# First-stage Fourier calls of later batches, placed behind the group steps of their unit

## The chip, the cores and the metric

The kernel runs on one core of one Trainium2 chip. The metric is the device time of one execution in microseconds (us). Before the change three runs took 1579.62, 1581.74 and 1581.88 us; their median is 1581.74 us.

Engines are called PE (matrix multiply), PEld (its weight load), DVE (vector), ACT (scalar and activation), POOL and SP. SP here only issues DMA transfers, and a DMA waits in its issuer's queue behind everything that was issued before it; the same holds for the few transfers that ACT issues.

## What is computed

The reference takes x (8 batches of 3072 x 256) through three parts, shortened here:

```
X = rfft(x, axis=1)                        # per batch, over 3072
Y = X @ (w_r + i*w_i) + (b_r + i*b_i)      # complex mix of the 256 columns
Y = soft_threshold(Y, 0.01)                # real and imaginary part
y = irfft(Y)                               # back to 3072 x 256 per batch
r = relu(y @ w_in);  z = (s*r*r + b) @ w_out          # 256 -> 2048 -> 256
logits = z @ w_gate;  e = argmax(logits)              # 8 experts, capacity 768 each
out[i] = softmax_weight * (relu(z_i @ w1[e]) @ w2[e]) # kept rows; other rows are zero
```

## The kernel before

**Loops and units.** The main part runs one loop per batch, b = 0 to 7, of 64 *units* each (k = 0 to 63). A unit (`s_unit`, from line 746) does one sixteenth-part of the first wide product of one eighth of batch b: four matmuls `ph` (L755), a relu on ACT into `r` (L760) and a square on DVE into `qb` (L761). Its PSUM tile comes from a pool "h" of two buffers. After each unit the kernel runs the list of small pieces that stands at that unit in a table (`slot`). The order of the pieces in a unit's list is the order in which the program put them there, so PE, ACT and SP meet them in that order, and each of these engines works strictly in order.

**The pieces.** While loop b multiplies batch b, the pieces bring the next batches through the Fourier part.

- *First-stage calls* (`f1_mm`, 8 per batch) belong to batch b+2 and are in loops 0 to 5. One call is four matmuls `pz` (L237; eight records in the trace, as each is split in two), which take a tile of the same pool "h"; an ACT copy to `z` (L241); four stores `zd` of 96 KB from SP (L245); and two loads of x of 192 KB from SP (L221) for the call two further on. The last two calls of loop 5 load no x. Eight calls for batch 1 are in loop 0 as well, at even units from 6.
- *Group steps* (`group_items`) belong to batch b+1. The first piece loads two `zp` (L265, 256 KB from SP). After it, steps of two kinds alternate: one loads the next `zp`, mixes (`pmx`, L358), thresholds on DVE and multiplies back (`pi`, L394, then a copy `v` on ACT and a store `vd` that ACT issues); the other mixes (`pmx`) and transforms (`pf`, L276, which reads `zp`). In loops 1 to 6 the first piece is at unit 0, the second (loads only) at unit 2, the first `pf` at unit 3, and the steps go on at every second or third unit to unit 50. The steps of units 46 and 50 hold nothing, that of unit 48 only the `pi`. In loop 0 they are at units 24 to 52.
- *Inverse pieces* (`i2_items`) are at units 8i+4 and 8i+5: they read `u` (L403, 384 KB from SP), multiply (`pi`, L415), and store `ad` (L435) from SP. The first two `u` of the next batch are loaded at unit 53 and the first is used at unit 57 (INV0_AT).
- At units 8i+2 there is a logit product `lg` (L775, L778), at units 8i+4 a transpose `plt` (L799), and every fifth unit SP issues a store of zeros to `out` (L1927).

**What sets the order.** No scheduler: the numbers F1_AT, GROUPS_FROM, GROUPS_TO, INV_LOAD_AT and the order of the `put` calls (lines 1896 to 1916) decide it. `put(at, items, per)` puts item n at unit int(at + n*per). Before the change, with F1_AT = 2, the calls of loops 1 to 5 are at units 2, 9, 17, 25, 33, 40, 48, 56 and those of loop 0 at 24, 29, ... 59; they are put in before the group steps of the same unit.

Of the kernel before, what the change touches and what calls it, by code (L numbers as in the profile page):

```python
# [132 lines left out]
GROUPS_TO = 50  # L133
INV_LOAD_AT = 53
INV0_AT = (57, 57, 61)
F1_AT = 2
ZERO_AT = tuple(range(5, 65, 5))
LOGIT_LAG = 3
FIRST_LAG = 13
# [12 lines left out]
class Kern:  # L152
# [1608 lines left out]
    def run(self):  # L1761
        tc, nc, B = self.tc, self.nc, self.B
# [4 lines left out]
        with ExitStack() as es, tc.manual_schedule():  # L1767
# [79 lines left out]
            def fetch(m):  # L1847
                t = self.wk.tile([128, 2, C], F32, tag=("kw", "kw2")[m % 2], name="ga", bufs=1)
                src = self.ad.rearrange("(k j a q g) c -> g j a k q c", j=2, a=4, q=4, g=NK * B)
                for j in range(2):  # L1850
                    for a in range(4):
                        nc.sync.dma_start(out=t[32 * a:32 * a + 32, j], in_=src[m, j, a])
                ga[m] = [t[:, j] for j in range(2)]
# [4 lines left out]
            for b in range(B):  # L1858
# [35 lines left out]
                def put(at, items, per=1.0):  # L1894
                    for n, f in enumerate(items):
                        slot.setdefault(int(at + n * per), []).append(f)
                if b + 1 < B:
                    if b == 0:
                        put(4, [lambda c=c: self.x_ahead(8 + c) for c in range(XP)], 0.5)
                        put(6, self.f1_items(1), 2)  # L1900
                    if b + 2 < B:
                        at = F1_AT if b else 24
                        put(at, self.f1_items(b + 2), (64 - at) / 8)
                    gi = self.group_items(b + 1)
                    s0 = GROUPS_FROM if b else 26
                    put(s0 - 2, gi[:1])
                    ge = GROUPS_TO if b else 52
                    put(s0, gi[1:], (ge - s0) / (len(gi) - 2))
                    put(INV_LOAD_AT, [lambda: self.i2_load(b + 1, 0), lambda: self.i2_load(b + 1, 1)], 0)
                    for at, f in zip(INV0_AT, self.i2_items(b + 1, 0)):  # L1910
                        put(at, [f])
                for i in range(7):
                    if i < 6:
                        put(8 * i, [lambda i=i: self.i2_load(b, i + 2)])
                    for at, f in zip(INV_AT, self.i2_items(b, i + 1)):
                        put(8 * i + at, [f])
                if b == 1:
                    for m, i in enumerate(XB_AT):
                        put(8 * i, [lambda m=m: fetch(m)])
# [70 lines left out]
```

## Time and profile before

| | before |
|---|---|
| median of three runs | 1581.74 us |
| the profiled execution | 1585.16 us |
| its span in the trace | 1583.1 us |
| PE busy | 1423.6 us (90%), 9725 instructions |
| DVE busy | 944.8 us (60%) |
| ACT busy | 793.1 us (50%) |
| POOL busy | 266.8 us (17%) |
| mean DMA rate | 145 GB/s |
| calls of `pz` (L237) | 480 records, 73.5 us busy |

The profile page gives busy times by engine and by group; the trace below it gives every instruction with its start, and, in brackets, how long its engine had been idle in front of it and which instruction ended that. Times in the trace count from the start of the span. The profiled execution is 2.06 us longer than its span. Loop 1 of the kernel runs from about 327 us to 552 us (it holds more work than the others), loop 2 to 706, loop 3 to 848, loop 4 to 991, loop 5 to 1133 us.

### The profile page before, as it was taken

To read this page: it belongs to the slowest core of one execution; us is meant where nothing else is said; L and a number is where in the kernel's file an instruction comes from. 1 tells how busy PE (TensorE), PEld (TensorE's weight loads), DVE (VectorE), ACT (ScalarE), POOL (GpSimd) and SP (SyncE) were. 2 spreads that over 40 slices of the span, in tenths; PEclk is the share of its full clock that TensorE was granted. 3 is DMA by queue.
4 is the path that set the end of the run, shared out by engine and by line. 5 is a ranking of instruction groups with operands and counts; after the bars stand their busy time and mean duration, and the time that the engine had idled before them with its cause. 6 is when DMAs were issued, how large, how long until landed. Compare 5 with 4: busy or idle time off the path is not lost.

```text
span 1583.1 us, 26459 instructions
## 1 busy us (share of the span) xinstructions
PE 1423.6 (90%) x9725; PEld 1195.4 (76%) x9725; DVE 944.8 (60%) x2078; ACT 793.1 (50%) x1196; POOL 266.8 (17%) x235
## 2 busy tenths in 40 slices
PE   5996869999998889999999999999999978998974
PEld 3985648878777668778877887888789867988863
DVE  1776427756554687757666675766677685552410
ACT  1334534465444545575557556655745675642311
POOL 0444200000000002212001201200120152223020
PEclk8898879999999999999999999999999999999987
DMA  7726566584444446466547555554543456530052
GB/s 207 243 87 196 143 181 172 153 218 134 146 140 126 129 128 160 126 168 161 160 117 200 143 144 163 151 164 127 156 118 109 119 148 195 158 94 21 11 198 99
DMA packets 270291, 230.03 MB, mean 145 GB/s; under 512 B 122526, under 2 KB 230816, under 8 KB 270145
## 3 DMA queue, kind: packets, MB, share of 16 engines
q1 hardware_dynamic: 252352, 200.14, 45.6%
q10 hardware_dynamic: 13968, 25.20, 4.5%
q0 software_dynamic: 3824, 2.82, 0.7%
q8 instruction: 81, 1.33, 0.4%
q14 instruction: 66, 0.53, 0.1%
HBM read 114.18 MB, written 114.09 MB: 144 GB/s over the span
## 4 chain that ended last, share of the span: by engine, by line
PE 69%; DVE 10%; ACT 6%; DMA 5%; issue 4%; SPq 2%; POOL 1%; another core or an unknown queue 1%; ACTq 0%; POOLq 0%; DVEq 0%
PE ph L755 16%; PE pmx L358 15%; PE pi L415 5%; PE pf L276 5%; PE pi L394 4%; PE pz L237 4%; PE phx L972 3%; ACT r L760 3%; PE lg L775 3%; PE ya L1434 2%; PE ph L1481 2%; DVE qb L761 2%; PE plt L799 2%; PE ya L987 1%; PE po L1491 1%
## 5 line engine op out<-in xcount | busy, mean ns | idle before, releaser
L755 PE MATMUL ph<-ah,win 128*128 128x384 f32 (+1 forms) x2048 | 449.1, 352 | 16.8 <-ACT r L760 13.6
L760 ACT ACTIVATE r<-ph 128x768 bf16<-128x768 f32 (+1 forms) x512 | 388.1, 784 | 146.8 <-PE ph L755 89.5
L761 DVE TENSOR_TENSOR qb<-r 128x768 bf16<-128x768 bf16 (+1 forms) x512 | 281.5, 554 | 211.7 <-ACT r L760 201.3
L755 PEld LDWEIGHTS ph<-ah,win 128*128 128x128 f32 x2048 | 339.6, 191 | 74.7 <-ACT r L760 44.4
L358 PE MATMUL pmx<-wm,l 128*128 128x256 f32 x1196 | 296.4, 387 | 10.4 <-DVE at L431 5.5
L358 PEld LDWEIGHTS pmx<-wm,l 128*128 128x128 f32 x1196 | 223.0, 192 | 53.5 <-DVE at L431 8.2
L421 POOL TENSOR_TENSOR asq<-ah 128x768 bf16<-128x768 f32 x64 | 96.7, 1511 | 968.7 <-ACT ah L417 888.5
L415 PE MATMUL pi<-f1t,u 96*128 96x96 f32 x1024 | 134.3, 283 | 6.5 <-DMA u<-vd 3.5
L415 PEld LDWEIGHTS pi<-f1t,u 96*128 96x128 f32 x1024 | 130.8, 198 | 11.5 <-issue 5.8
L284 ACT COPY l<-pf 128x512 f32<-128x512 f32 x84 | 49.2, 586 | 152.2 <-PE pf L276 145.2
L396 ACT COPY v<-pi 128x512 f32<-128x512 f32 x96 | 56.4, 588 | 100.6 <-PE pi L394 97.9
L276 PEld LDWEIGHTS pf<-d,zp 128*128 128x128 f32 x672 | 89.6, 195 | 15.2 <-issue 8.2
L394 PE MATMUL pi<-t,e 128*128 128x256 f32 x384 | 99.2, 381 | 0.7 <-DVE t L353 0.7
L276 PE MATMUL pf<-d,zp 128*128 128x128 f32 x672 | 90.6, 279 | 10.3 <-DMA zp<-zd 10.3
L237 PE MATMUL pz<-x,f 48*64 48x512 f32 x480 | 73.5, 645 | 17.8 <-ACT r L760 9.3
L417 ACT CAST ah<-pi 128x384 fp32r<-128x384 f32 x128 | 61.0, 479 | 52.8 <-PE pi L415 51.8
L431 DVE STREAM_TRANSPOSE at<-pi 128x384 f32<-128x384 f32 x128 | 74.2, 580 | 20.3 <-ACT ah L417 12.9
L394 PEld LDWEIGHTS pi<-t,e 128*128 128x128 f32 x384 | 72.3, 190 | 15.1 <-DVE qb L761 3.2
L909 POOL DMA_INDIRECT list<-c,x x64 | 65.5, 1024 | 80.9 <-DVE c L905 64.7
L285 DVE TENSOR_TENSOR l<-pf,l 128x256 f32<-128x256 f32 x84 | 35.6, 424 | 68.8 <-ACT l L284 65.9
L353 DVE TENSOR_TENSOR t<-t,cl 128x512 f32<-128x512 f32 x96 | 73.4, 765 | 3.3
L241 ACT COPY z<-pz 128x1024 f32<-128x1024 f32 x56 | 56.7, 1012 | 29.4 <-PE pz L237 16.9
(409 smaller groups left out, 1826.1 us busy)
## 6 DMA issues: line engine op xcount, KB each, us to landing
zd<-z SPq DMA_DIRECT2D x256, 96.0 KB
zp<-zd SPq DMA_DIRECT2D x96, 256.0 KB
vd<-v ACTq DMA_DIRECT2D x96, 256.0 KB
u<-vd SPq DMA_DIRECT2D x64, 384.0 KB
ad<-at SPq DMA_DIRECT2D x256, 96.0 KB
out<-zero SPq DMA_DIRECT2D x96, 256.0 KB
x<-x SPq DMA_DIRECT2D x120, 192.0 KB
sd<-stage SPq DMA_DIRECT2D x32, 256.0 KB
```

The costliest lines, as they stand in the source:

```text
L237: nc.tensor.matmul(ps[r][64 * k:64 * k + 64, :], self.f1[h], xs[k][h].rearrange("p a c -> p (a c)"), start=True, stop=True, skip_group_che ...
L276: nc.tensor.matmul(pv[:, h, :, gi * 64:gi * 64 + 64], zp[:, gi, h * 128:(h + 1) * 128], self.d[:, 2 * p + gi, :].rearrange("p (t m) -> p t ...
L353: nc.vector.tensor_tensor(out=t, in0=t, in1=cl, op=ALU.subtract)
L358: self.nc.tensor.matmul(o, part(h), w[:, h], start=start and h == 0, stop=stop and h == 1, skip_group_check=True)
L394: nc.tensor.matmul(ps[:, gi * C:(gi + 1) * C], self.e[:, 2 * p + gi], t[:, gi * C:(gi + 1) * C], start=True, stop=True)
L415: nc.tensor.matmul(ps[:, :TC].rearrange("p (a n) -> p a n", n=4)[:, :, n], u[:, n, h::2], self.f1t, start=True, stop=True)
L421: nc.gpsimd.tensor_tensor(out=self.asq[b, i], in0=af, in1=af, op=ALU.mult)
L431: nc.vector.transpose(out=self.ar[:, :, :, h], in_=self.at.pop((b, i, h))[:, :TC].rearrange("p (g c) -> p g c", c=32))
L755: nc.tensor.matmul(ps[:, j, :n], self.win[:, k, f], ah[:, k, t0:], start=(k == 0), stop=(k == 1))
L760: nc.scalar.activation(out=r, in_=ps[:, :, :n], func=AF.Relu)
L761: nc.vector.tensor_tensor(out=q, in0=r, in1=r, op=ALU.mult)
L909: self.nc.gpsimd.indirect_dma_start(out=self.lists[n], out_offset=bass.IndirectOffsetOnAxis(ap=x[:, n:n + 1], axis=0), in_=c[:, n:n + 1], ...
```

## The change

F1_AT becomes a list of eight units, the calls are put in after all other pieces of the unit, and loop 0 keeps its units (24, 29, ... 59) but has the calls behind the other pieces too. Counts and shapes stay as they are. In loops 1 to 5 a call goes from unit 2, 9, 17, 25, 33, 40, 48, 56 to unit 3, 10, 18, 25, 31, 38, 45, 50.

```diff
-F1_AT = 2
+F1_AT = (3, 10, 18, 25, 31, 38, 45, 50)
...
                     if b == 0:
                         put(4, [lambda c=c: self.x_ahead(8 + c) for c in range(XP)], 0.5)
                         put(6, self.f1_items(1), 2)
-                    if b + 2 < B:
-                        at = F1_AT if b else 24
-                        put(at, self.f1_items(b + 2), (64 - at) / 8)
                     gi = self.group_items(b + 1)
...
                     for at, f in zip(INV_AT, self.i2_items(b, i + 1)):
                         put(8 * i + at, [f])
+                if b + 2 < B:
+                    for at, f in zip(F1_AT if b else range(24, 64, 5), self.f1_items(b + 2)):
+                        put(at, [f])
```

On PE, in the later loops around units 32 to 34 (`ph` of two units in one row; `pmx` and `pi` are of the group steps, `pz` is the call):

```order
 L358 MATMUL pmx<-wm_152,l 128x256 x2
 L394 MATMUL pi_6253<-t,e 128x256 x2
-L755 MATMUL ph<-ah,win 128x384 x8
-L237 MATMUL pz<-x,f_108 64x512 x4
+L237 MATMUL pz<-x,f_108 64x512 x4
+L755 MATMUL ph<-ah,win 128x384 x8
 L358 MATMUL pmx<-wm_151,l 128x256 x2
 L358 MATMUL pmx<-wm_150,l 128x256 x2
```

The call stood behind two units and in front of the mixes of a step; now it stands behind the `pi` of the step of unit 31 and in front of the two units.

On SP in loop 0, about unit 24, before (the stores `zd` and loads `x` are those of a call, `zp` the first loads of the group steps):

```order
L1927 DMA out<-zero 256x1x256
L435 DMA ad<-at 32x12x64 x4
L245 DMA zd<-z 48x2x256 x4
L221 DMA x<-x 48x1024 x2
L265 DMA zp<-zd 128x512 x2
L403 DMA u<-vd_84 96x4x256
```

and after:

```order
L1927 DMA out<-zero 256x1x256
L435 DMA ad<-at 32x12x64 x4
L265 DMA zp<-zd 128x512 x2
L403 DMA u<-vd_84 96x4x256
L245 DMA zd<-z 48x2x256 x4
L221 DMA x<-x 48x1024 x2
```

The six transfers of the call went from in front of the `zp` loads to behind them and behind the load of `u`.

On SP in loop 3, units 45 to 53, before (the last row is the load of the first two `u` of the next batch):

```order
L435 DMA ad<-at 32x12x64 x4
L1927 DMA out<-zero 256x1x256
L245 DMA zd<-z 48x2x256 x4
L221 DMA x<-x 48x1024 x2
L1927 DMA out<-zero 256x1x256
L403 DMA u<-vd_88 96x4x256 x2
```

and after:

```order
L435 DMA ad<-at 32x12x64 x4
L245 DMA zd<-z 48x2x256 x4
L221 DMA x<-x 48x1024 x2
L1927 DMA out<-zero 256x1x256
L245 DMA zd<-z 48x2x256 x4
L221 DMA x<-x 48x1024 x2
L1927 DMA out<-zero 256x1x256
L403 DMA u<-vd_88 96x4x256 x2
```

The call that stood behind the two `u` loads (unit 56) is now in front of them, so the transfers of two calls instead of one lie between `ad` and `u`.

## Rows read from the trace of the kernel before

**Rows 1.** Stretches: microseconds, then busy time (count) per engine, granted clock, DMA share, GB/s.

```profile
706.00:848.00 142.00, 137.57 (x919) 114.88 (x918) 95.45 (x205) 85.02 (x121) 20.02 (x16) 1.00 0.58 156
828.00:832.00 4.00, 4.00 (x37) 3.07 (x35) 1.21 (x3) 3.54 (x6) 0.00 (x0) 1.00 0.91 253
```

**Rows 2.** PE timeline, loop 5: start, duration, engine, line, operation; idle in brackets.

```profile
1044.60 1.75 PE L755 MATMUL ph<-ah,win 128*128 128x384 f32 x8
1046.19 1.89 PE L358 MATMUL pmx<-wm,l 128*128 128x256 f32 x8
1047.92 1.05 PE L276 MATMUL pf<-d,zp 128*128 128x128 f32 x8
...
1088.86 1.74 PE L755 MATMUL ph<-ah,win 128*128 128x384 f32 x8
1091.15 1.09 PE L237 MATMUL pz<-x,f 48*64 48x512 f32 x8 [0.55 <-ACT r L760]
1092.17 1.99 PE L358 MATMUL pmx<-wm,l 128*128 128x256 f32 x8
1094.00 1.05 PE L276 MATMUL pf<-d,zp 128*128 128x128 f32 x8
```

**Rows 3.** PE timeline, unit 17 of loop 3, and two units together in loop 4.

```profile
744.98 0.94 PE L755 MATMUL ph<-ah,win 128*128 128x384 f32 x4
...
747.67 1.03 PE L358 MATMUL pmx<-wm,l 128*128 128x256 f32 x4
...
861.16 1.64 PE L755 MATMUL ph<-ah,win 128*128 128x384 f32 x8
862.63 1.03 PE L358 MATMUL pmx<-wm,l 128*128 128x256 f32 x4
```

**Rows 4.** Timelines of SP (SPq) and PE at units 0 to 3 of loops 1, 2, 3.

```profile
330.95 0.96 SPq L265 DMA_DIRECT2D zp<-zd  x2
333.93 1.16 PE L276 MATMUL pf<-d,zp 128*128 128x128 f32 x8 [1.57 <-DMA zp<-zd]
...
552.34 0.97 SPq L265 DMA_DIRECT2D zp<-zd  x2
557.19 1.05 PE L276 MATMUL pf<-d,zp 128*128 128x128 f32 x8
...
707.84 0.97 SPq L265 DMA_DIRECT2D zp<-zd  x2
708.56 1.09 PE L237 MATMUL pz<-x,f 48*64 48x512 f32 x8 [0.19 <-ACT r L760]
709.58 0.83 PE L775 MATMUL lg<-qb,wogd 128*32 128x384 bf16 x16
711.31 1.05 PE L276 MATMUL pf<-d,zp 128*128 128x128 f32 x8
```

**Rows 5.** PE timeline: a wait at unit 48 of loop 3, one at unit 25 of loop 5.

```profile
824.83 0.96 PE L755 MATMUL ph<-ah,win 128*128 128x384 f32 x4 [0.55 <-ACT r L760]
...
1050.58 1.09 PE L237 MATMUL pz<-x,f 48*64 48x512 f32 x8 [0.21 <-ACT r L760]
```

**Rows 6.** Timelines of SP and PE in loop 0, about unit 24.

```profile
217.90 1.88 SPq L245 DMA_DIRECT2D zd<-z  x4
...
220.79 0.90 SPq L265 DMA_DIRECT2D zp<-zd  x2
...
225.16 2.04 PE L276 MATMUL pf<-d,zp 128*128 128x128 f32 x8 [8.03 <-DMA zp<-zd]
```

**Rows 7.** Timelines of SP and PE, units 48 to 57 of loops 3 and 4.

```profile
828.77 2.73 SPq L245 DMA_DIRECT2D zd<-z  x4
832.25 0.80 SPq L221 DMA_DIRECT2D x<-x  x2
833.73 1.12 SPq L403 DMA_DIRECT2D u<-vd  x2
839.53 2.01 PE L415 MATMUL pi<-f1t,u 96*128 96x96 f32 x16
...
976.58 1.11 SPq L403 DMA_DIRECT2D u<-vd  x2
982.71 1.51 PE L415 MATMUL pi<-f1t,u 96*128 96x96 f32 x11 [1.28 <-DMA u<-vd]
```

## The prediction

> **What bounds the kernel now.** I read the busy times by engine first, then one loop of the later batches as a stretch. In loop 3 PE is busy for 137.57 of 142 us at a granted clock of 1.00 (2.4 GHz), ACT and DVE for 85 and 95 us [rows 1]. So PE's own order of work sets the pace: what a change of order is worth is what it does to the seams between PE's pieces and to the few waits that PE still has. The reader should look for two things in the PE timeline: how much later the next piece starts when a call stands in a place, and the bracket in front of an instruction.
>
> A call costs PE more than its own stream. In loop 5 two units, a mix and the next transform take 1047.92 − 1044.60 = 3.32 us from the first `ph` to `pf`; with a call between the units and the mix it is 1094.00 − 1088.86 = 5.14 us, of which 0.55 is a wait for ACT [rows 2]. So the call costs 5.14 − 0.55 − 3.32 = 1.27 us, though from `pz` to the next piece it is only 1092.17 − 1091.15 = 1.02. The rest lies in its seams: the mix behind it lasts 1.83 to the next start, against 1.73, and the `ph` in front of it gives way later. Between two units, where the unit holds no step, the call costs (747.67 − 744.98) − (862.63 − 861.16) = 2.69 − 1.47 = 1.22 us [rows 3]. In front of the logit product it is 709.58 − 708.56 = 1.02 [rows 4].
>
> **The change, part by part.** Durations are those of the profiled execution, so the sum is made against its 1583.1 us of span and 1585.16 us in all (2.06 us lie around the span), 3.42 us above the median of the three runs. The differences are then applied to the median.
>
> *Seams, loops 1 to 5.* Before, four of the eight calls stand in front of a step's matmuls (units 25, 33, 40, 48), three between units (9, 17, 56), and one in front of `lg` (unit 2): 4 × 1.27 + 3 × 1.22 + 1.02 = 9.76 us. After, all stand behind their step: five in front of the next unit's `ph` (3, 25, 31, 38, 45) and three in front of `lg` (10, 18, 50): 5 × 1.22 + 3 × 1.02 = 9.16. The trace has no call behind a `pf` or a `pi`; nearest are the two seams just named. The saving is 0.6 per loop, 3.0 us in five loops. Bounds: nothing, if the seam to the step costs the same from its other side, and 9.76 − 8 × 1.02 = 1.6 per loop if a call costs 1.02 everywhere, so 0 to 8 us. I take 3.0, since it is made of measured seams.
>
> *The wait for ACT at a call.* A call takes a buffer of the pool that the units use, and must wait until the relu of the unit two before is done. These waits are 0.19 at unit 2 [rows 4], 0.21 at unit 25 [rows 5] and 0.55 where two or three units come close together [rows 2, 5]; with 0.55 at units 33, 40 and 48, and 0.2 at unit 56 as at 2 and 25, that is 0.19 + 0.21 + 3 × 0.55 + 0.2 = 2.25 per loop. After, a call directly behind a step has the step's matmuls as cover for the relu, but the two units behind it come one call earlier to their own buffers. I take 0.40, the middle of 0.21 and 0.55, at three units (31, 38, 45), 0.55 at unit 50 and 0.20 once: 1.95, a gain of 0.3 per loop, 1.5 us in all. Bounds per loop: +1.5 if all of the old waits return and the copy of `z` delays the next relu besides, and −2.25 if all go.
>
> *Loop 0.* The units stay, only the order within them turns. The largest single wait here is PE's 8.03 us for the first `zp` [rows 6]. Its load is issued at 220.79, behind the four stores and two loads of the call at unit 24, which begin at 217.90. After the change it takes their place: 220.79 − 217.90 = 2.9 us sooner, and PE ends its wait that much sooner, if nothing but `zp` holds it. Five of the eight calls lie in units with a step's matmuls; at 0.12 each for the seam that is 0.6. Sum −3.5 us; bounds 0 (the time is lost again later, since the next `zp` loads keep PE waiting) and −5 (the load also lands faster: it takes 225.16 − 220.79 = 4.37 us here against 2.98 below).
>
> *The first `zp` of a loop.* Where a call goes away in front of unit 3, PE comes there sooner, and the load does not. In loop 1 it takes 333.93 − 330.95 = 2.98 us and PE already waits 1.57 [rows 4]: all of the 1.02 that the call gave as cover is added. In loop 3 PE arrives 711.31 − 707.84 = 3.47 us behind the issue, without a wait: 0.49 to spare; without the call at unit 2 (1.02, and its wait of 0.19) it arrives 1.21 sooner and waits 1.21 − 0.49 = 0.72. Loops 4 and 5 have the same places; I take 0.72 for each. Loop 2 has 557.19 − 552.34 = 4.85 us and so room for it. Sum 1.02 + 3 × 0.72 = +3.2 us; bounds 0 (the load lands sooner when no call stores beside it) and 6 (five times 1.21).
>
> *The loads of `u` at unit 53.* Now the transfers of the call of unit 50 stand in front of them, and those of the call of unit 45 too, so six more than before: four `zd` and two x. In loop 3 the two loads are issued at 833.73 and PE's `pi` starts at 839.53 without a wait, 5.80 us later; in loop 4 the same takes 982.71 − 976.58 = 6.13 and PE already waits 1.28 [rows 7]. What the room in loop 3 is cannot be seen; from nothing to 5.80 − 2.98, the time of the smaller load. I take 0.5, since loop 4 lies so near. How much later are the loads issued? Upper end: four stores at 2.73 and two loads at 0.80, with short gaps, 3.6 us. Lower end: nothing, if SP has time between its rows, for it mostly waits for `z`. I take 2.0: SP has gaps (its stores end at 828.77 + 2.73 = 831.50, and the next row begins at 832.25), and the first call's six fall partly into them. Loops 2 and 3: 2.0 − 0.5 = 1.5 each; loop 4: all 2.0; loop 5, whose last two calls load no x: 0.5; loop 1, where PE has more work before unit 57: nothing. Sum +5.5 us; bounds 0 and 12.
>
> The Trainium skill, "DMA: Bandwidth & Descriptors", section "Issuing engines are not separate DMA queues", says that all DMAs run on the same 16 engines and interleave. What the rows show that bears on it is that in the four us in which these transfers run the DMA share is 0.91 at 253 GB/s, against 0.58 in the loop [rows 1]. [...]
>
> Sum: −3.0 − 1.5 − 3.5 + 3.2 + 5.5 = +0.7 us. Span 1583.8, profiled execution 1585.9, median 1582.4.
>
> **The rivals.**
>
> *A. The `u` loads land in time: faster.* SP issues the first call's six transfers while it would have waited for the second call's `z`, and the room in loops 2 to 5 takes the rest. For it: SP's queue is not full, and no wait at `pi` is seen in loop 3. Against it: loop 4 waits already. Then the 5.5 fall away: −4.8 us, 1576.9.
>
> *B. The `u` loads are late by the full six transfers: slower.* The place is the first `pi` at unit 57 in loops 2 to 5, the price 3.6 − 0.5 = 3.1 in loops 2 and 3, 3.6 in loop 4 and 2.2 in loop 5, together 12.0 instead of 5.5: +7.2 us, 1588.9. It decides from a delay of about 2.8 us on; below that the sum stays within a measurement's reach. For it: the crowded DMA in that stretch. Against it: SP's gaps.
>
> *C. The change doesn't do what it says: the seams cost the same on either side of a step.* Then the 3.0 are not had: +3.7 us, 1585.4. For it: the mix behind a call lasts 0.10 longer, so it is the change of the shape that costs, and that comes twice at any place. Against it: the calls between units are cheaper than those in front of a mix. The Trainium skill, "TensorE: Matmul & The Clock Gate", section "The mechanism", says that a weight load overlaps a running matmul only where the row groups differ, which would make the seam a matter of the shapes; the 1.22 and 1.27 are near enough to agree, the 1.02 in front of `lg` isn't.
>
> **How the numbers follow.** A measurement of this kernel tells about 0.2%, 3.2 us, from no change: the bounds are 1578.6 and 1584.9. Forecast 0.42, rival A 0.32, rival B 0.17, rival C 0.09. Of the forecast's cases, with its terms a few us off in either direction, 0.03 count as faster and 0.02 as slower; of C 0.04 count as no change. Faster: 0.32 + 0.03 = 0.35. Slower: 0.17 + 0.05 + 0.02 = 0.24. No change: 0.41. The range reaches from A with another 1.4 us of seams or waits gone, 1575.5, to B, 1588.9, since both hold much of the chance. The forecast's own range is 1579 to 1586.
>
> **What would show it.** In the changed profile: `pf` at unit 3 waits about 2.6 us for `zp` in loop 1 and 0.7 in loops 3 to 5; the wait in loop 0 is about 5.1 instead of 8.03; the calls in front of `lg` cost 1.02 with no dearer seam at the step; `pi` at unit 57 waits 1.5 us for `u` in loops 2 and 3 and about 3.3 in loop 4. The forecast is wrong if the `u` load is not waited for (A), if its wait is over 3 us in each loop (B), if the loop 0 gain is given back to the next `zp`, or if the waits for ACT at the calls grow instead of falling.

## The result, and the profile after

| | before | after |
|---|---|---|
| median of five runs | 1581.68 us | 1597.19 us |
| range of the runs | 1579.62 to 1581.88 | 1594.50 to 1601.28 |
| span of the profiled execution | 1583.1 us | 1592.7 us |
| PE waits for `u` (L415), whole execution | 3.5 us in 2 places | 10.3 us in 5 places |

The change makes the kernel slower: the ratio to before is 1.0113, interval 1.0089 to 1.0137. The forecast was 1582.4 with a range to 1588.9, so the time lies outside the range, on the side of rival B and beyond it.

The most useful view is a ledger: the start of the same `ph` (first of a unit) in both traces, and by how much the difference of the two grows in each stretch.

| stretch | forecast, us | traces, us |
|---|---|---|
| loop 0 up to unit 57 | −3.5 | −5.1 |
| loop 0, units 57 to 60 | 0 | +3.1 |
| units 0 to 4, loops 1 to 5 (`zp`) | +3.2 | +6.4 |
| units 4 to 14, loops 1 to 5 | 0 | +2.9 |
| units 14 to 57 (in loop 1 to 60; seams, waits for ACT) | −4.5 | −3.1 |
| units 57 to 60, loops 2 to 5 (`u`) | +5.5 | +12.4 |
| loops 6 and 7 | 0 | −1.8 |
| together, to unit 60 of loop 7 | +0.7 | +14.8 |

The spans differ by only 9.6 us, since the stretch behind unit 60 of loop 7, which the change doesn't touch, took 183.9 us in the profiled execution of before and 178.6 after; over the kernels below it is anything from 176.8 to 183.9, so this difference lies within the scatter. The 14.8 up to there agrees with the medians, which differ by 15.5. Two more entries are scatter, at least in part: 0.8 of loop 0's 5.1 us are there at unit 24 already, before the first call that changed its place, and loops 6 and 7 hold no moved call.

Units 50 to 60 of loop 3 after, first SP's issues and then PE; they answer to [rows 7].

```profile
831.85 1.91 SPq L435 DMA_DIRECT2D ad<-at  x4
833.86 2.36 SPq L245 DMA_DIRECT2D zd<-z  x4
836.32 1.15 SPq L221 DMA_DIRECT2D x<-x  x2
...
838.16 2.01 SPq L245 DMA_DIRECT2D zd<-z  x4
840.26 0.85 SPq L221 DMA_DIRECT2D x<-x  x2
...
841.74 1.16 SPq L403 DMA_DIRECT2D u<-vd  x2
...
844.62 0.96 PE L755 MATMUL ph<-ah,win 128*128 128x384 f32 x4 [0.19 <-ACT r L760]
847.25 2.33 PE L415 MATMUL pi<-f1t,u 96*128 96x96 f32 x16 [1.67 <-DMA u<-vd]
849.28 1.63 PE L755 MATMUL ph<-ah,win 128*128 128x384 f32 x4
850.84 1.47 PE L775 MATMUL lg<-qb,wogd 128*32 128x384 bf16 x16
```

Two calls' transfers stand ahead of `u`, and `pi` waits 1.67 us where it waited for nothing. The two rows below it are the surprise: four `ph` matmuls take 1.63 us and the logit product 1.47, which elsewhere take 0.94 to 0.97 and 0.83 [rows 3, 4, 5]. PE runs at half rate there. The stretches show it (columns as in [rows 1]): first loop 3 before, behind its `pi`, and the stretch behind loop 4's wait of 1.28 us,

```profile
842.00:845.00 3.00, 3.00 (x33) 2.25 (x31) 1.17 (x3) 2.63 (x5) 1.64 (x1) 1.00 0.82 216
...
985.00:988.00 3.00, 3.00 (x32) 2.23 (x31) 1.12 (x2) 2.63 (x4) 1.38 (x1) 1.00 0.87 241
```

and after, behind the waits of loops 3, 2, 4 and 0:

```profile
849.00:852.00 3.00, 3.00 (x23) 2.01 (x24) 0.80 (x2) 1.29 (x2) 0.00 (x0) 0.50 0.31 104
702.00:705.00 3.00, 3.00 (x22) 2.15 (x24) 0.58 (x1) 1.47 (x3) 0.00 (x0) 0.53 0.21 69
997.00:1000.00 3.00, 3.00 (x18) 2.35 (x21) 0.58 (x1) 0.97 (x3) 0.00 (x0) 0.50 0.07 23
316.00:319.00 3.00, 3.00 (x17) 2.79 (x16) 0.58 (x1) 0.96 (x2) 0.00 (x0) 0.58 1.09 299
```

The granted clock is 1.00 (2.4 GHz) before and about 0.5 (1.2 GHz) after. Read in stretches of 2 us from 300 to 1160 us, the time lost to a lower clock (the sum of 2 us times one minus the granted clock) is 5.1 us in three falls before and 13.7 us in eight falls after. They come in equal steps: one fall loses 1.7 us. The same sum from the start to unit 60 of loop 7 is 41.0 us before and 49.5 after, so of the 14.8 us lost, 8.5 are the clock's.

The first `pf` of loops 0, 1 and 3, which answer to [rows 6] and [rows 4]:

```profile
220.16 2.05 PE L276 MATMUL pf<-d,zp 128*128 128x128 f32 x8 [3.83 <-DMA zp<-zd]
...
332.20 1.16 PE L276 MATMUL pf<-d,zp 128*128 128x128 f32 x8 [2.92 <-DMA zp<-zd]
333.30 1.81 PE L237 MATMUL pz<-x,f 48*64 48x512 f32 x8
...
715.72 1.16 PE L276 MATMUL pf<-d,zp 128*128 128x128 f32 x8 [0.86 <-DMA zp<-zd]
```

Loop 0's wait fell from 8.03 to 3.83 us, more than forecast (2.9). In loop 1 the wait grew from 1.57 to 2.92, and `pz` behind it lasts 1.81 instead of 1.09: the clock again. In loop 3 a wait of 0.86 is new.

A wait that nobody had foreseen is at unit 10 of loop 3:

```profile
729.12 0.94 PE L755 MATMUL ph<-ah,win 128*128 128x384 f32 x4
730.95 1.97 PE L358 MATMUL pmx<-wm,l 128*128 128x256 f32 x8 [0.89 <-DVE t L382]
```

The call that stood at unit 9 was cover for DVE, which must finish with a tile before this mix can start; a run below tests that.

The seams, at unit 31 of loop 3 after, which answer to [rows 2, 3]:

```profile
789.60 1.03 PE L394 MATMUL pi<-t,e 128*128 128x256 f32 x4
790.56 1.09 PE L237 MATMUL pz<-x,f 48*64 48x512 f32 x8
791.58 0.97 PE L755 MATMUL ph<-ah,win 128*128 128x384 f32 x4
793.13 0.97 PE L755 MATMUL ph<-ah,win 128*128 128x384 f32 x4 [0.58 <-ACT z L241]
793.93 1.89 PE L358 MATMUL pmx<-wm,l 128*128 128x256 f32 x8
```

The call itself no longer waits, but the second unit behind it now waits for ACT's copy of `z`, 0.58 us. And from `pi` to `ph` it takes 791.58 − 789.60 = 1.98 us, where without a call it is 1088.86 − 1088.18 = 0.68, in loop 5 of before:

```profile
1088.18 1.03 PE L394 MATMUL pi<-t,e 128*128 128x256 f32 x4
1088.86 1.74 PE L755 MATMUL ph<-ah,win 128*128 128x384 f32 x8
```

The call costs 1.30 behind a `pi`, as much as the 1.27 in front of a mix.

### The profile page after: what moved, and what is told of

It reads as the page before. It is cut to its first block, busy times and chain, and to the rows that moved or that the text cites. A ratio compares the mean times of both kernels' runs of the same rounds, so it can differ in the third digit from the quotient of the medians.

```text
span 1592.7 us, 26452 instructions
## 1 busy us (share of the span) xinstructions
PE 1434.4 (90%) x9725; PEld 1199.5 (75%) x9725; DVE 949.3 (60%) x2078; ACT 795.1 (50%) x1196; POOL 264.3 (17%) x235
## 5 line engine op out<-in xcount | busy, mean ns | idle before, releaser
L755 PE MATMUL ph<-ah,win 128*128 128x384 f32 (+1 forms) x2048 | 454.3, 356 | 16.4 <-ACT r L760 9.6
L755 PEld LDWEIGHTS ph<-ah,win 128*128 128x128 f32 x2048 | 343.3, 194 | 90.6 <-ACT r L760 30.7
L415 PE MATMUL pi<-f1t,u 96*128 96x96 f32 x1024 | 137.5, 287 | 13.3 <-DMA u<-vd 10.3
L415 PEld LDWEIGHTS pi<-f1t,u 96*128 96x128 f32 x1024 | 133.6, 202 | 19.0 <-issue 7.1
L276 PEld LDWEIGHTS pf<-d,zp 128*128 128x128 f32 x672 | 88.5, 193 | 17.1 <-DMA zp<-zd 8.9
L431 DVE STREAM_TRANSPOSE at<-pi 128x384 f32<-128x384 f32 x128 | 74.2, 580 | 29.0 <-DMA ad<-at 13.7
```

The lines of the kernel that those rows point to most:

```text
L276: nc.tensor.matmul(pv[:, h, :, gi * 64:gi * 64 + 64], zp[:, gi, h * 128:(h + 1) * 128], self.d[:, 2 * p + gi, :].rearrange("p (t m) -> p t ...
L415: nc.tensor.matmul(ps[:, :TC].rearrange("p (a n) -> p a n", n=4)[:, :, n], u[:, n, h::2], self.f1t, start=True, stop=True)
L431: nc.vector.transpose(out=self.ar[:, :, :, h], in_=self.at.pop((b, i, h))[:, :TC].rearrange("p (g c) -> p g c", c=32))
L755: nc.tensor.matmul(ps[:, j, :n], self.win[:, k, f], ah[:, k, t0:], start=(k == 0), stop=(k == 1))
```

## The experiments

Two theories were set against each other first: that the new places cost (P), or that standing behind a step costs (O). All ratios are to the kernel before on the same chip; there were three sets, with medians of before of 1582.08, 1584.07 and 1576.64 us. The expected times were written with a before of about 1582 us in mind; where before took another time, above all in the third set, a result is held against them by its ratio.

**Order alone.** The calls behind, at the units of before:

```diff
-F1_AT = (3, 10, 18, 25, 31, 38, 45, 50)
+F1_AT = (2, 9, 17, 25, 33, 40, 48, 56)
```

> The calls stand behind the other pieces of their unit, as after the change, but in loops 1 to 5 at the units of before (2, 9, 17, 25, 33, 40, 48, 56). Theory P (the places cost, not the order within a unit): the waits for zp at unit 3 and for u at unit 57 in loops 1 to 5 are those of before, loop 0 keeps what it has after the change (about 2 us less than before), and the median is 1578 to 1582. Rival O (standing behind a step costs, by dearer seams and later stores): the loss stays, 1590 to 1598.

Measured: 1574.37 us, ratio 0.9941 (0.9925 to 0.9958). O falls; the order is even a gain, and more than P had it. In the trace there is no wait for `u` in loops 1 to 5 and none for `zp` in loops 2 to 5; loop 4's 1.28 of before is gone as well:

```profile
974.56 0.97 PE L755 MATMUL ph<-ah,win 128*128 128x384 f32 x4
975.37 2.01 PE L415 MATMUL pi<-f1t,u 96*128 96x96 f32 x16
```

**Place alone.** The list of new units in before's position:

```diff
-F1_AT = 2
+F1_AT = (3, 10, 18, 25, 31, 38, 45, 50)
...
-                        at = F1_AT if b else 24
-                        put(at, self.f1_items(b + 2), (64 - at) / 8)
+                        for at, f in zip(F1_AT if b else range(24, 64, 5), self.f1_items(b + 2)):
+                            put(at, [f])
```

> The calls stand in front of the other pieces of their unit, as before the change, but in loops 1 to 5 at the new units (3, 10, 18, 25, 31, 38, 45, 50); loop 0 is as before. Theory P: PE waits for u at unit 57 in loops 2 to 4 as after the change (1.7 to 3 us), and for zp at unit 3 less, since the call is in front of pf there and covers about 1 us; 1590 to 1597. Rival O: about as before, 1580 to 1584.

Measured: 1587.36, ratio 1.0030 (1.0009 to 1.0050). The interval corresponds to 1583 to 1590, between O's times and P's: the loss is smaller than P had it, but the kernel is slower than before, as P says. The waits for `u` were shorter than P had them, 0.72, 0.44 and 1.99 us in loops 2 to 4; only the longest was followed by a low clock. So the places cost, and more so together with the new order.

**The loads of `u` first.**

```diff
-                    put(INV_LOAD_AT, [lambda: self.i2_load(b + 1, 0), lambda: self.i2_load(b + 1, 1)], 0)
+                    put(50 if b else INV_LOAD_AT, [lambda: self.i2_load(b + 1, 0), lambda: self.i2_load(b + 1, 1)], 0)
```

> As after the change, but in loops 1 to 6 the two loads of u are issued at unit 50 instead of 53, in front of the stores and loads of the call at unit 50. Theory Q (SP's queue order delays u): the waits at unit 57 in loops 2 to 4 go, and with them the low granted clock behind them, 3.5 to 4.8 us in each of these loops; 1583 to 1587. Rival V (the transfers' volume delays u, wherever they stand in the queue): u still lands late, 1591 to 1597.

Measured: 1586.82, ratio 1.0033 (1.0014 to 1.0051), 0.8% below the changed kernel's 1.0113. SP at unit 50 of loop 3 and PE at unit 57:

```profile
826.12 2.37 SPq L245 DMA_DIRECT2D zd<-z  x4
...
830.35 1.11 SPq L403 DMA_DIRECT2D u<-vd  x2
831.55 1.97 SPq L245 DMA_DIRECT2D zd<-z  x4
...
837.71 2.01 PE L415 MATMUL pi<-f1t,u 96*128 96x96 f32 x16
839.50 0.94 PE L755 MATMUL ph<-ah,win 128*128 128x384 f32 x4
```

`pi` has no wait and the `ph` behind it is at full rate, though the same transfers run in the same microseconds (a share of 1.01 from 830 to 836 us): it is the place in SP's queue, theory Q, not the volume alone. The loads also moved from unit 53 to 50, but SP's own time explains the gain: they now leave 6.56 us before unit 57 instead of 2.88, and of these 3.68 us the six transfers and the store of zeros that stood in front of them after the change take 3.58 (838.16 to 841.74 in the rows above).

**The first call at unit 2, and the second at unit 9**, one at a time:

```diff
-F1_AT = (3, 10, 18, 25, 31, 38, 45, 50)
+F1_AT = (2, 10, 18, 25, 31, 38, 45, 50)
```

> As after the change, but the first call of loops 1 to 5 is at unit 2 again (behind the loads of that unit). Theory P: the wait for zp at unit 3 goes back to 1.6 us in loop 1 and to none in loops 2 to 5, with the low granted clock in loop 1: 0.8 to 1.2 us less in loops 2 to 5 and about 3 us in loop 1, 1589 to 1592. Rival (the call's cost only moves, its cover is worth nothing): 1595 to 1598.

Measured: 1590.65, ratio 1.0054 (1.0035 to 1.0072). `zp` isn't waited for in loops 2 to 5, and 1.94 us in loop 1, with no fall of the clock; units 0 to 4 of the five loops together differ by +1.1 from before instead of +6.4. As P says.

```diff
-F1_AT = (3, 10, 18, 25, 31, 38, 45, 50)
+F1_AT = (3, 9, 18, 25, 31, 38, 45, 50)
```

> As after the change, but the second call of loops 1 to 5 is at unit 9 again. If this call covers DVE's work for the mix at unit 10, the wait of 0.9 us there goes, and units 4 to 14 of loops 3 to 5 take 0.5 to 1 us less each: 1593 to 1596 and no wait for DVE at unit 10 in the trace. Rival (the cover is worth nothing, another wait comes for it at unit 13): 1596 to 1598.

Measured: 1596.45 in the third set, ratio 1.0107 (1.0075 to 1.0139), not to be told from the changed kernel's 1.0113. The mix at unit 10 of loop 3 has no wait:

```profile
733.21 0.94 PE L755 MATMUL ph<-ah,win 128*128 128x384 f32 x4
733.99 1.89 PE L358 MATMUL pmx<-wm,l 128*128 128x256 f32 x8
```

and units 4 to 14 of loops 3 to 5 are 1.0 us shorter each (−0.45, −0.45 and +0.03 against before, instead of +0.55, +0.55 and +1.02). By its ratio it would be 1599 in the first set, above both ranges. In the traced execution the clock took the gain back: 20.5 us are lost to it instead of 13.7, with two falls behind `u` in loops 2 and 3 instead of one. So the cover is shown by the trace at its place and not by the total.

**All three repairs**, units 2 and 9 for the first calls and the loads of `u` at 50 (the edits above together):

> As after the change, with three repairs in loops 1 to 5: the first call at unit 2, the second at unit 9, and the loads of u at unit 50. If the waits for zp (about 7 us with the clock), for DVE at unit 10 (about 2 us) and for u in loops 1 to 4 (about 14 us with the clock) explain the loss, 1573 to 1577. If the other moved calls (17 to 18, 33 to 31, 40 to 38, 48 to 45, 56 to 50) cost by themselves, over 1580.

Measured: 1578.08, ratio 0.9966 (0.9947 to 0.9985), some 23 us below the changed kernel's ratio. In microseconds it is 1 us above the first range; by its ratio, 1576.7, it is in it. Between the changed kernel and order alone lie 27 us (1.0113 and 0.9941), so the three places account for most of the loss; the rest, some 4 us, is what the other moved calls can have cost, and it is not clear of noise, since the intervals of the two kernels overlap.

**The clock by itself.** Four matmuls without use in the wait:

```diff
+WARM_U = 4
...
+                    if b in (2, 3, 4):
+                        put(57, [lambda: self.warm(WARM_U)])
                     for at, f in zip(INV0_AT, self.i2_items(b + 1, 0)):
```

> As after the change, with four more matmuls (128x256, on a tile of zeros, their output is not used) on PE at unit 57 of loops 2, 3 and 4, between the unit and the inverse piece that waits for u. They last about 1.6 us, less than the waits of 1.67 to 3.0 there. Theory C (PE standing idle for u makes the granted clock fall behind the wait): the clock stays at 1.00 in the 4 us behind the wait, u lands as before, and units 57 to 60 take 1 to 2 us less in each of the three loops, 3 to 6 us in all; 1591 to 1594. Rival (the clock falls for another reason, or the matmuls cost what they save): 1596 to 1599, the clock at 0.5 behind the wait.

Measured: 1613.71, ratio 1.0201 (1.0174 to 1.0228): a miss in the total. At the place itself it came as theory C says. Loop 3 of this kernel (its lines are one further on):

```profile
851.87 1.89 PE L444 MATMUL warm<-zero 128*128 128x256 f32 x8
854.32 2.10 PE L416 MATMUL pi<-f1t,u 96*128 96x96 f32 x16 [0.56 <-DMA u<-vd]
856.19 0.95 PE L756 MATMUL ph<-ah,win 128*128 128x384 f32 x4
```

and the stretch behind it:

```profile
857.00:861.00 4.00, 4.00 (x37) 3.32 (x37) 1.84 (x4) 3.33 (x5) 1.67 (x1) 1.00 0.01 5
```

The clock stays at 1.00 in loops 2 to 4, and units 57 to 60 lose 2.2, 2.5 and 1.8 us against before, where the changed kernel loses 4.2, 3.5 and 4.8: 5.9 us back. What is lost elsewhere is a new wait of 2.1 us for DVE at unit 13 of loops 3 to 5, and falls of the clock in loops 1, 2, 4 and 5, 17.1 us between 300 and 1160 us. The four matmuls take a PSUM tile of the steps' pool, so the tiles' turn is shifted; that this makes the wait at unit 13 is argued, not shown. A like wait of 2.19 us stands at unit 13 of loop 3 in the kernel with three repairs, which has no such matmuls, and loop 1, where five of the ten falls are, has none either.

**A wait made without any moved call.** Before, with the `u` loads two units later:

```diff
-INV_LOAD_AT = 53
+INV_LOAD_AT = 55
```

> The kernel before, with nothing changed but that the two loads of u are issued at unit 55 instead of 53, behind the four stores ad; the calls stand where they stood. Theory C (PE idle for u, by whatever cause, makes the granted clock fall): in loops 2 to 4 PE waits 4 to 7 us for u at unit 57 and the clock is at 0.5 behind it, 1.7 us or twice that lost on top of each wait; with loops 0 and 5 1605 to 1616. Rival (the falls belong to the moved calls): the clock stays at 1.00 behind the waits, and only their length is lost, 1600 to 1606.

Measured: 1626.67, ratio 1.0310 (1.0273 to 1.0348). In loop 2:

```profile
713.12 3.70 PE L415 MATMUL pi<-f1t,u 96*128 96x96 f32 x16 [3.47 <-DMA u<-vd]
716.53 1.63 PE L755 MATMUL ph<-ah,win 128*128 128x384 f32 x4
```

and as a stretch:

```profile
713.00:717.00 4.00, 3.88 (x18) 3.91 (x19) 0.58 (x1) 0.62 (x2) 0.00 (x0) 0.50 1.05 294
```

PE waits 3.1 to 3.5 us in loops 1 to 5, less than expected, 7.5 in loop 0 and 4.2 in loop 6, and 23.9 us are lost to the clock between 300 and 1160 us instead of 5.1. In loop 2 units 57 to 60 lose 6.3 us for a wait of 3.5. No call was moved here, so the falls belong to the wait. The total is beyond the range that C gave: C counted loops 0 and 2 to 5, but loops 1 and 6 wait too and lose 5.8 and 7.3 us between units 57 and 60, and loop 0 loses 11.3.

**Loop 0.** Loop 0's part of the change alone, on before:

```diff
-                    if b + 2 < B:
+                    if b and b + 2 < B:
...
+                if b == 0:
+                    put(24, self.f1_items(2), 5)
```

> As before the change, but in loop 0 the calls of units 24, 29, ... 59 stand behind the other pieces, as after. From the trace after: about 5 us gained at the first zp load, about 3 to 4 given back at unit 57, where PE then waits for u with a lower clock behind it. 1578 to 1582. The forecast's own term for loop 0 alone would give 1578.

Measured: 1578.93, ratio 0.9970 (0.9952 to 0.9989). 5.4 us are gained up to unit 57 and 3.15 given back between units 57 and 60, with a wait of 1.38 for `u`: 2.2 us net at the end of loop 0, of which 0.4 are there before the first moved call. So the trace has what was expected, and not the forecast's 3.5; the total, 1.7 to 7.6 us below before, is too wide to tell the two apart.

Then with order alone, and other units in loop 0, to keep the gain:

```diff
-                    for at, f in zip(F1_AT if b else range(24, 64, 5), self.f1_items(b + 2)):
+                    for at, f in zip(F1_AT if b else (24, 29, 34, 39, 44, 53, 56, 59), self.f1_items(b + 2)):
```

> As the kernel with the calls behind the other pieces at the units of before, but in loop 0 the calls of units 49 and 54 stand at 53 and 56, so that their transfers are behind the loads of u. Theory G (loop 0's gain is given back because the last store of v and the loads of u share the DMA engines with the call of unit 49): the wait for u at unit 57 of loop 0 and the low clock behind it go, about 4 us; 1569 to 1572. Rival (the loads of u are late for another reason, the stores of v themselves): 1573 to 1576.

Measured: 1574.05, ratio 0.9947 (0.9926 to 0.9967), in the rival's range and not in G's. The traced execution was the slowest of the kernel's seven (1584.51). In it the wait for `u` is gone, but the call of unit 59 comes so soon behind the others that it waits for its x, and the clock falls all the same:

```profile
320.80 2.68 PE L237 MATMUL pz<-x,f 48*64 48x512 f32 x8 [1.67 <-DMA x<-x]
```

and the stretch behind it:

```profile
322.00:326.00 4.00, 4.00 (x19) 2.56 (x13) 0.70 (x2) 1.61 (x2) 0.33 (x1) 0.50 0.57 156
```

With earlier units instead:

```diff
-                    for at, f in zip(F1_AT if b else range(24, 64, 5), self.f1_items(b + 2)):
+                    for at, f in zip(F1_AT if b else (24, 29, 34, 38, 42, 46, 54, 59), self.f1_items(b + 2)):
```

> As the kernel with the calls behind the other pieces at the units of before, but in loop 0 the calls of units 39, 44 and 49 stand at 38, 42 and 46, so that their transfers are done when the last store of v and the loads of u are issued. If the crowd of transfers holds u back in loop 0, its wait at unit 57 (1.0 us) and the two falls of the clock behind it (1.7 us each) go: 1570 to 1573. If the last store of v comes late by itself: 1573 to 1577.

Measured: 1570.83 in the third set, ratio 0.9953 (0.9936 to 0.9969). In microseconds that is in the range of the first theory, but before was faster there too; by its ratio it is 1574.6, in the range of the second. So the total does not decide. The trace speaks for the first: the gain of loop 0 stays, `pi` at unit 57 does not wait, units 57 to 60 add 0.0, and only two falls are left between 300 and 1160 us (3.4 us). By the ratio it can't be told from order alone (0.9941) or from the late calls (0.9947). All three are faster than both kernels, by about 0.5% against before and 1.7% against after.

## Why the prediction was wrong, by its own steps

- *The loads of `u` at unit 53.* This is the step that failed, and the largest part of the miss: 6.9 of the 14.1 us between the forecast's +0.7 and the ledger's +14.8. The mechanism was right: the loads are issued 2.3 us later against `ad` (9.89 instead of 7.55 us behind it in loop 3; I took 2.0), and the waits grew by 2.45, 1.67, 1.72 and 0 us in loops 2 to 5, 5.8 in all where I had 5.5. The term was mis-sized because a wait was charged with its own length only. Behind it PE ran at half rate: units 57 to 60 took +4.2, +3.5, +4.8 and 0 us, 12.4 in all. The upper bound of 12 left the clock out too.
- *Loop 0.* The `zp` wait went by 4.2 us (I had 2.9), but the sum took it as kept. PE comes 5.1 us sooner to unit 57, `u` is issued only 3.4 us sooner (311.45 instead of 314.87), and 3.1 us are given back: a wait of 1.35 and one fall. `u` reads what the last store `vd` writes, and from that store's issue to the load's it took 4.2 us after and 2.5 before; that the load waited for the store to land is likely, but the trace does not name what released it. The forecast looked for that at the next `zp`; it came one step further on.
- *The first `zp` of a loop.* Waits of +1.35 in loop 1 (1.02 forecast), 1.14 in loop 2 (none forecast), 0.86, 0.87 and 0.60 in loops 3 to 5 (0.72 each): 4.8 instead of 3.2. The ledger has 6.4: 0.9 more are the part of loop 1's fall that lies in front of unit 4, and 0.1 to 0.2 in each other loop have no wait to explain them. Loop 2 lost its room because SP issued the load 0.9 us later (553.23 instead of 552.34), behind four stores `ad` that took 3.47 us on SP instead of 1.90.
- *Seams and waits for ACT.* −4.5 forecast, −3.1 measured, and 1.7 of that is a fall of the clock in loop 1 (510 to 516 us) that before has and after hasn't. So some 1.4 are left. Rival C was right for `pi` (1.30 behind it). The waits for ACT in front of `pz` in loops 1 to 5 fell from 8.0 to 2.9 us, but those in front of `ph` grew from 5.7 to 7.9. The prediction had put the old waits at 2.25 us per loop, where the trace has 1.6; the 0.55 that it read at unit 48 stands in front of a `ph` there, not of the call [rows 5]. The sentence on weight loads beside C isn't borne out by [rows 1]: PE and PEld are busy for 137.57 and 114.88 of 142 us, so most weight loads run beside a matmul, though most of the matmuls there use all 128 rows. That order alone gives more is shown by its run.
- *Cover that I did not look for.* The call at unit 9 hid DVE's work for the mix at unit 10; without it units 4 to 14 took +0.55, +0.55 and +1.02 us in loops 3 to 5, where the forecast has nothing.
- *The rivals.* None of them came true as a whole. A fails, since `u` is waited for. B asked for a delay of 3.6 us and waits of over 3 us in each loop; the delay was 2.3 and the waits 2.45, 1.67, 3.00 and 0 us, nearer to the forecast's own. That the measured time lies beyond B's 1588.9 comes of the clock, which no case priced, and of the other terms above.

## What to carry to other kernels

Where PE is the bound, a piece of its work that stands in front of a wait is cover: before moving it, list what it covers (a load, another engine's work) at the place that it leaves, and what queues behind its DMAs at the place where it goes. Price a new wait on PE not by its length alone: look in the trace at the granted clock behind waits of that size. And change order and place one at a time; here the order is worth about half a per cent, and the new places, behind the steps, took that three times over.

## What the runs showed of the hardware

Waits of 1.0 us (loop 0 of order alone) to 3.0 us on an otherwise busy PE were followed by a granted clock of 0.50, and each fall lost 1.7 us. Others were not followed by one: 1.28 us in loop 4 of before, 1.57 in loop 1 of before [rows 4], 1.94 in loop 1 of the kernel with its first call at unit 2. So the length of the wait alone doesn't decide it. One wait was followed by one fall, by two (loop 4 after: 3.4 us lost behind 3.0 of waiting) or by the loss of four (6.8 us from 330 to 344 us, behind 2.71 of waiting for `zp` in loop 1 of the kernel with four matmuls without use), and the same place took one fall in one kernel and two in another, which can make a few us of scatter between like kernels; what decides it stays open. The Trainium skill, "TensorE: Matmul & The Clock Gate", section "What's actually happening", has the low clock as the default which activity lifts; the run with four matmuls without use agrees: the clock was 1.00 behind the places that they filled.
